# One attention and mixture-of-experts kernel: its order planner gets measured transfer lengths with a margin, its zero products another rule, and its order a new search

## The chip, the core and the metric

The program runs on one core of a Trainium2 chip. The core has five engines that work side by side and each take their instructions in program order: PE (matrix products), DVE (vector), ACT (scalar functions), POOL (general), and SP, which here only issues DMA transfers. The metric is the device time of one execution in microseconds (us). The kernel before was timed three times: 987.84, 989.49 and 993.25 us, median 989.49.

## The reference: what is computed

Attention over 8 batches, 12 heads, 448 positions and head width 64, with q and k normalised; its output, taken as 3584 tokens of 768 values, goes into a mixture of 8 experts, where each token uses the one expert of the greatest logit.

```python
q_n, k_n = (rmsnorm(q, g_q), rmsnorm(k, g_k))
scores = scale * np.matmul(q_n, k_n.transpose(0, 1, 3, 2))
scores = scores - np.max(scores, axis=-1, keepdims=True)
attn = np.exp(scores)
attn = attn / (np.sum(attn, axis=-1, keepdims=True) + 1e-09)
attn_out = np.matmul(attn, v)
...
x = np.ascontiguousarray(attn_out.transpose(0, 2, 1, 3)).reshape(B * S, H * D)
logits = x @ w_gate
e_idx = np.argmax(logits, axis=1)
...
for e in range(E):
    mask = e_idx == e
    h = np.maximum(x[mask] @ w1[e], 0.0)
    out[mask] = gate_w[mask, None] * eom[mask, e, None] * (h @ w2[e])
```

## The kernel before, in words

**Pairs of heads.** Attention is done in 48 pairs of heads, six to a batch. `pair_ops(i)` (before.py from line 509) writes down the steps of pair i, each with a name, an engine, a duration in ns that the planner counts with, the steps it needs, and the buffers it takes. The names are used below: `Lt` loads q and k (tile qkt); `sq`, `mh`, `ms` square and sum them; four small steps per group of pairs make the factor y; `n` and `qg` scale qkt; `hi` and `lo` split it into two halves of 16 bits (tile X); `Th` and `Tl` are the DMA transposes of the two halves into tile ss; `M0` to `M3` are products for the row maxima (psM), which DVE reduces in `x0` to `x3` (tile Z); `NT` and `nt` turn the maxima round; `S0` to `S3` are the scores (pss), six big and eight small products each; `e`, `f` on ACT take their exponentials and `p` forms the low half pl; `Lv`, `vh`, `vl` load and split v (tile vf). `A0` to `A6` multiply the exponentials with v into the one bank bank_a; the division of a pair is `av1`, `av2`, `av` on DVE (tiles rc and xr). bank_a is held from A0 of a pair until its `av`, so A0 of the next pair waits for that division. `tr`, `th`, `lg`, `la` make the router's logits, and `r<b>` finds the slots of batch b's tokens.

**The planner.** `Order.run` plays all these steps through, engine by engine, with the durations written down. Whenever an engine is free it takes, of the steps whose needs, buffers and transfers are due, the one with the smallest key. Keys come from the pair's number plus the numbers of the tables ORDER and SHIFT; SECOND says, pair by pair, on which of two engines a step runs. The program is then written out in the order in which the planner took the steps. No time of the planner is measured; it only settles what stands before what. A transfer is counted as a latency (`lat`) and a length on one common queue (`xfer`).

**Zero products.** Where the planner finds PE without work for longer than 400 ns between two steps, `run` puts n = (wait - 400) / 30 small products of a zero tile (nil, 56 columns, line 1456) behind the earlier step; they write columns 456 to 511 of bank_a, which the pairs' products don't use. 80 larger products of zeros (`w`, line 444) may run at the start wherever nothing else is due.

**After attention.** The first expert's products (g1e, line 1251) are part of the same plan. They need the tokens of that expert: route of batch 6 (r6), four scatters into a table (tab), a load from it (tie), three gathers (xge), a split (x16e) and three transposes (xTe). From there on a fixed order handles the other experts.

## Time and profile before

| | |
|---|---|
| median of three timed executions | 989.49 us |
| the profiled execution, device time | 990.61 us |
| its span in the trace | 988.6 us |
| outside the span | 2.0 us |
| PE busy | 934.8 us (95%) |
| DVE busy | 631.9 us (64%) |
| ACT, POOL busy | 549.7, 418.2 us (56%, 42%) |
| granted PE clock, mean over the span | 0.985 of full |

The table is read as averages over unlike stages: the first expert's products begin at 524.67 us, and up to there PE shares its time with three nearly full engines; behind it PE works with almost no pause. The busy time of PE holds the zero products too.

### The profile page before, as it was taken

The numbers are of one execution on the slowest core, as the hardware profiler recorded it, in microseconds if no ns is written. First come the engines' busy times: TensorE is split into PE (matmuls) and PEld (weight loads), VectorE is DVE, ScalarE is ACT, GpSimd is POOL, SyncE is SP. The second block draws the span as 40 slices with busy tenths as digits, with TensorE's granted clock in tenths as the row PEclk, the third lists the DMA queues.
The fourth block names the chain that finished last, engine by engine and source line by source line (L and its number), as shares of the span: only waits on it lengthen the run. The fifth ranks groups of instructions, "written<-read, shape, count | busy, mean of one in ns | idle before, by whom it ended". The sixth has DMA issues, their size and how long they took to land. (4 is left out here: it accounts for less than half of the span.)

```text
span 988.6 us, 29294 instructions
## 1 busy us (share of the span) xinstructions
PE 934.8 (95%) x12747; PEld 671.4 (68%) x12747; DVE 631.9 (64%) x1064; ACT 549.7 (56%) x809; POOL 418.2 (42%) x314
## 2 busy tenths in 40 slices
PE   5998999998899999999899999999999999999997
PEld 2576777776677777777676686686776767666664
DVE  6889899888787889896575456428336263536210
ACT  5876979878768677674582445324234252535110
POOL 3656768884766958644641313112121111101101
PEclk7999999999889999998999999999999999999999
DMA  6776969868659576564866599949738486667201
GB/s 169 137 195 135 209 141 165 199 115 174 110 114 218 107 170 123 128 93 75 171 194 206 144 268 265 203 108 237 192 105 238 117 232 187 180 211 218 69 1 47
DMA packets 182544, 157.44 MB, mean 159 GB/s; under 512 B 152448, under 2 KB 160262, under 8 KB 176268
## 3 DMA queue, kind: packets, MB, share of 16 engines
q1 hardware_dynamic: 176652, 133.28, 57.8%
q0 software_dynamic: 5760, 22.25, 7.1%
q8 instruction: 102, 1.67, 0.7%
q14 instruction: 30, 0.25, 0.1%
HBM read 96.73 MB, written 22.59 MB: 121 GB/s over the span
## 5 line engine op out<-in xcount | busy, mean ns | idle before, releaser
L667 POOL TENSOR_TENSOR pl<-p,ph 128x896 f16<-128x896 f32 x79 | 149.8, 1903 | 112.5 <-ACT ph L662 45.1
L613 DVE TENSOR_REDUCE Z<-psM 128x2 f16<-128x896 f32 x168 | 178.3, 1086 | 21.1 <-PE psM L598 16.2
L699 PE MATMUL bank_a<-vf,pf 128*128 128x65 f32 (+1 forms) x896 | 149.5, 280 | 8.1 <-DVE xr L717 8.1
L1266 POOL DMA_INDIRECT out<-oe,tie x24 | 27.7, 1155 | 254.4 <-DVE oe L1288 232.9
L640 PE MATMUL pss<-ss 64*128 64x448 f16 (+1 forms) x1152 | 127.0, 358 | 7.8 <-DVE pl L667 3.1
L699 PEld LDWEIGHTS bank_a<-vf,pf 128*128 128x128 f32 (+1 forms) x896 | 110.1, 180 | 26.5 <-issue 11.3
L1251 PE MATMUL g1e<-xTe,w0he 128*128 128x384 f16 x384 | 125.2, 326 | 0.0
L1253 PE MATMUL g1e<-xTe,w0le 128*128 128x384 f16 x384 | 125.2, 326 | 0.0
L1252 PE MATMUL g1e<-xTe,w0he 128*128 128x384 f16 x384 | 125.2, 326 | 0.0
L703 PE MATMUL bank_a<-vh,pl 128*128 128x65 f16 (+1 forms) x1088 | 123.0, 195 | 1.7 <-issue 1.7
L703 PE MATMUL bank_a<-vh,ph 128*128 128x65 f16 (+1 forms) x1088 | 122.6, 196 | 0.0
L701 PE MATMUL bank_a<-vl,ph 128*128 128x64 f16 (+1 forms) x1088 | 122.4, 193 | 0.0
L662 ACT ACTIVATE ph<-pss 128x896 f16<-128x896 f32 x112 | 101.8, 922 | 17.2 <-PE pss L646 17.2
L703 PEld LDWEIGHTS <-ph 128*128 128x128 f16 (+1 forms) x1088 | 110.2, 117 | 0.0
L703 PEld LDWEIGHTS <-pl 128*128 128x128 f16 (+1 forms) x1088 | 90.7, 101 | 1.8 <-issue 1.8
L701 PEld LDWEIGHTS <-ph 128*128 128x128 f16 (+1 forms) x1088 | 90.7, 103 | 0.0
L652 ACT ACTIVATE pf<-pss,lnv 128x896 f32<-128x896 f32 x56 | 56.6, 1010 | 50.2 <-PE pss L646 47.0
L658 ACT ACTIVATE p<-pss 128x896 f32<-128x896 f32 x79 | 72.2, 920 | 15.1 <-PE pss L646 12.0
L1253 PEld LDWEIGHTS <-w0le 128*128 128x128 f16 x624 | 60.7, 98 | 24.8
L1251 PEld LDWEIGHTS <-w0he 128*128 128x128 f16 x624 | 60.7, 98 | 23.7
L1252 PEld LDWEIGHTS <-w0he 128*128 128x128 f16 x624 | 60.7, 98 | 23.6
L646 PEld LDWEIGHTS <-sel 64*128 64x128 f16 (+1 forms) x1536 | 53.2, 99 | 31.3 <-issue 3.3
(328 smaller groups left out, 2300.8 us busy)
## 6 DMA issues: line engine op xcount, KB each, us to landing
wste<-w SPq DMA_DIRECT2D x48, 1024.0 KB, 5.8
qkt<-qkt SPq DMA_DIRECT2D x48, 448.0 KB, 4.4
vf<-v SPq DMA_DIRECT2D x48, 260.0 KB, 3.4
xs<-xr SPq DMA_DIRECT2D x16, 576.0 KB, 3.5
ss<-X SPq DMA_TRANSPOSE x96, 4.3
xs<-xr SPq DMA_DIRECT2D x16, 96.0 KB, 4.3
tab<-val,slot POOLq DMA_INDIRECT x32, 4.9
xge<-xs,tie POOLq DMA_INDIRECT x24, 4.9
```

Source lines behind the costliest of these rows:

```text
L613: V.tensor_reduce(out=o, in_=m, op=ALU.max, axis=AX.X, negate=True)
L640: T.matmul(out, lhsT=side(wk, 1, h, 128 * u, n, x), rhs=side(wq, 0, h, 0, S, x), start=k == 0, stop=False)
L652: A.activation(out=t, in_=st[f"S{u}"], func=AF.Exp, bias=self.lnv)
L658: A.activation(out=t, in_=st[f"S{u}"], func=AF.Exp)
L662: A.activation(out=t, in_=st[f"S{u}"], func=AF.Exp)
L667: return (V if eng == DVE else Pl).tensor_tensor(out=t, in0=st[f"e{u}"], in1=at[f"ph{u}"], op=ALU.subtract)
L699: T.matmul(out, lhsT=st[f"pf{u}"][:, k, q], rhs=vf[:, jv, :], **go)
L701: T.matmul(out[:, 0:D], lhsT=at[f"ph{u}"][:, k, q], rhs=vl[:, jv, :], start=False, stop=False)
L703: T.matmul(out, lhsT=at[f"p{'hl'[w // 2]}{u}"][:, k, q], rhs=vh[:, jv, :], **go)
L1251: nc.tensor.matmul(o, lhsT=wh[:, sl], rhs=xT[:, 0, k, 0:n], start=k == 0, stop=False)
L1252: nc.tensor.matmul(o, lhsT=wh[:, sl], rhs=xT[:, 1, k, 0:n], start=False, stop=False)
L1253: q["mm"] = nc.tensor.matmul(o, lhsT=wl[:, sl], rhs=xT[:, 0, k, 0:n], start=False, stop=k == KD - 1)
```

## The change

The planner's rules and numbers change, and with them the order of nearly all steps before 524.67 us; the work of each step does not. Part by part:

- Transfers are counted longer in `lat` (`Lt`, `Th` 1400 ns more, `Lv`, `Tl` 1050 ns more, by the new table LATE) and with other lengths (`Lt` 1900 to 2450 and 1900 to 1700, `Th`, `Tl` 1700 to 2020 and 1250 to 1180, `Lv` 1200 to 765, `k.cst` 546 to 1600, the loads of weights `ld` 2000 to 2500 or 5000, the store `st`). Two durations change as well: `S3` 960 to 700, `lg` 380 to 460.
- Zero products are now put in only for waits of more than 800 ns, and never between a pair's last product A and its division: there they go behind the division (`pad`, in front of the next step).
- `k.zero`, which makes the zero tiles, waits for `ms.0`.
- ORDER, STICK, SECOND and SHIFT hold new numbers. SECOND moves steps between engines: by count, 14 half-tiles of `lo` and 7 `qg` go from DVE to POOL, 15 `th`, 8 `vh`, 2 `nt` from ACT to DVE, 3 `p` from POOL to DVE, 2 `sq` from ACT to POOL, and 2 `mh` more are made on POOL, each of which halves an `ms` on DVE.

```diff
-REST, BEAT = 400, 30
+REST, BEAT, GAP = 400, 30, 800
+LATE = dict(Lt=1400, Lv=1050, Th=1400, Tl=1050)
...
-    ("S0", 0.028, 0.084, 2293.989, 0.255),
+    ("S0", 0.087, 0.406, 914.631, 0.073),
...
-    "lo": "100010 110001 110110",
+    "lo": "100100 110000 111000",
...
-    "th": "001000 000111 010100",
+    "th": "011111 011111 000001",
...
-        op = dict(name=name, eng=eng, ns=ns, after=after, key=key, fn=fn, bufs=bufs, lat=ns if lat is None else lat, xfer=xfer, port=port)
+        op = dict(name=name, eng=eng, ns=ns, after=after, key=key, fn=fn, bufs=bufs, lat=ns if lat is None else lat + LATE.get(name[:2], 0), xfer=xfer, port=port)
...
-        last = None
+        last, held = None, {}
         for o in out:
-            if o["eng"] == PE:
-                if last and last["until"] >= WARM:
-                    last["still"] = max(0, int((self.start[o["name"]] - last["until"] - REST) / BEAT))
-                last = o
+            if o["eng"] != PE:
+                continue
+            nm, r = o["name"].split(".")
+            if last and last["until"] >= WARM:
+                a, b = last["until"], self.start[o["name"]]
+                end = done.get(f"av.{held['i']}", 0) if held.get("n") == 7 else 0
+                side = "pad" if end > a else "still"
+                n = int((b - max(a, end) - REST) / BEAT)
+                if n > (GAP - REST) / BEAT:
+                    last[side] = n
+                    if side == "pad":
+                        o["pad"] = last.pop("pad")
+            if nm[0] == "A":
+                held = {"i": r, "n": held["n"] + 1 if held.get("i") == r else 1}
+            last = o
...
-        self.order.add("k.zero", DVE, 330, [], -20, lambda: [nc.vector.memset(x, 0.0) for x in (self.zero, self.nil)])
+        self.order.add("k.zero", DVE, 330, ["ms.0"], -20, lambda: [nc.vector.memset(x, 0.0) for x in (self.zero, self.nil)])
...
-        do("Th", SP, 1235, "hi", lambda: flip(0), f"ss:S0,S1,S2,M0,M1,M2", 1700, 1250, more=["k.edges"])
+        do("Th", SP, 1235, "hi", lambda: flip(0), f"ss:S0,S1,S2,M0,M1,M2", 2020, 1180, more=["k.edges"])
...
-            do(f"S{u}", PE, 768 if u < 3 else 960, "Tl", lambda u=u: Sc(u), f"s:{'p' if near else 'e'}{u}" + ("" if u in whole or near else f",f{u}"), more=more)
+            do(f"S{u}", PE, 768 if u < 3 else 700, "Tl", lambda u=u: Sc(u), f"s:{'p' if near else 'e'}{u}" + ("" if u in whole or near else f",f{u}"), more=more)
...
-        do("Lv", SP, 475, "", lambda: self.loadv(i), f"vf:{As}", 2100, 1200, more=[f"Th.{i}"] * (i < 4) + [f"Lv.{i - 1}"] * (i > 0))
+        do("Lv", SP, 475, "", lambda: self.loadv(i), f"vf:{As}", 2100, 765, more=[f"Th.{i}"] * (i < 4) + [f"Lv.{i - 1}"] * (i > 0))
...
+        def still(n):
+            for _ in range(n):
+                nc.tensor.matmul(self.bank_a[:, 456:512], lhsT=self.nil, rhs=self.nil[:, 0:56], start=True, stop=True)
+
         for o in self.order.run():
+            still(o.get("pad", 0))
             o["ins"] = o["fn"]()
-            if o.get("still"):
-                for _ in range(o["still"]):
-                    nc.tensor.matmul(self.bank_a[:, 456:512], lhsT=self.nil, rhs=self.nil[:, 0:56], start=True, stop=True)
+            still(o.get("still", 0))
```

The tables' numbers tell a reader nothing; what they make of the order is seen at three places. In the program before stand 849 zero products at 41 places, 21 of them with more than 13 each, which is what the new limit of 800 ns asks for; in the changed program stand 382 at 8 places.

The first place is PE where the products of pair 0 end (vh_114, pl_3 are its operands; psM_4 are the maxima of pair 4). Before:

```order
L703 LDWEIGHTS pl_3_592
L703 MATMUL bank_a<-vh_114,pl_3_592 128x65
L1456 LDWEIGHTS nil
L1456 MATMUL bank_a<-nil 128x56
...
L598 LDWEIGHTS ss_111
L598 MATMUL psM_4_888<-ss_111 128x448
```

The zero products there are 52. After (psM_5 are the maxima of pair 5, pss_2 the scores S2 of pair 3):

```order
L715 LDWEIGHTS pl_3_899
L715 MATMUL bank_a<-vh_114,pl_3_899 128x65
L610 LDWEIGHTS ss_107
L610 MATMUL psM_5_1088<-ss_107 128x448
...
L652 LDWEIGHTS ss_110
L652 MATMUL pss_2_1092<-ss_110 128x448
```

The zero products are gone from between the last product and the division, and real products of later pairs stand in their place.

The second place is DVE at the start, from the maxima of pair 0 (psM0_0) to those of pair 1 (psM2_1 and so on). Before:

```order
L613 TENSOR_REDUCE Z0_112<-psM0_0_252 128x2
L495 SCALAR_TENSOR_TENSOR y02_262<-psy02_263,y02_262 128x28
L558 TENSOR_REDUCE ms03_294<-sq4_278 128x14
L613 TENSOR_REDUCE Z0_112<-psM3_1_303 128x2
L613 TENSOR_REDUCE Z0_112<-psM2_1_308 128x2
L613 TENSOR_REDUCE Z0_112<-psM1_1_330 128x2
```

After:

```order
L625 TENSOR_REDUCE Z0_112<-psM1_0_256 128x2
L570 TENSOR_REDUCE ms02_286<-sq2_222 128x14
L570 TENSOR_REDUCE ms02_286<-sq3_278 128x14
L512 SCALAR_TENSOR_TENSOR psy02_305<-psy02_305,mm02_302 128x28
L686 TENSOR_SCALAR vh0_114<-vf0_245 128x6x64
L507 SCALAR_TENSOR_TENSOR y02_304<-psy02_305,y02_304 128x28
L690 SCALAR_TENSOR_TENSOR vl0_318<-vf0_245,vh0_114 128x384
L574 TENSOR_TENSOR qkt3_224<-qkt3_224,y02_304 128x896
L574 TENSOR_TENSOR qkt2_188<-qkt2_188,y02_304 128x896
L625 TENSOR_REDUCE Z0_112<-psM2_1_334 128x2
L625 TENSOR_REDUCE Z0_112<-psM3_1_339 128x2
```

Two sums ms, the scalings n of pairs 2 and 3 and the split of v of pair 0 now stand ahead of pair 1's maxima, which NT of pair 0 needs.

The third place is SP where attention passes into the experts (vf46, vf47 are loads of v, wste0_0 to wste0_3 of the first expert's weights, tie0 the load of its token list). Before:

```order
L1122 DMA wste0_0_10612<-w 128x2048
L468 DMA vf46_10719<-v 128x520
L1122 ISA
L1122 DMA wste0_1_10836<-w 128x2048
L1187 ISA
L1187 DMA tie0_10858<-tab_87 128x6
L468 DMA vf47_10881<-v 128x520
```

After:

```order
L480 DMA vf46_10243<-v 128x520
L1121 TENSOR_LOAD est0_126
L1121 ISA x2
L1134 ISA
L1134 DMA wste0_0_10284<-w 128x2048
L480 DMA vf47_10480<-v 128x520
L1199 ISA
L1199 DMA tie0_10500<-tab_87 128x6
L1134 ISA
L1134 DMA wste0_1_10505<-w 128x2048
```

The last load of v now stands ahead of the token list, and the second weight load behind it.

## Rows read from the trace of the kernel before

**Rows 1.** The page's head and part 1, and the PE clock of its part 2.

```profile
span 988.6 us, 29294 instructions
...
PE 934.8 (95%) x12747; PEld 671.4 (68%) x12747; DVE 631.9 (64%) x1064; ACT 549.7 (56%) x809; POOL 418.2 (42%) x314
...
PEclk7999999999889999998999999999999999999999
```

**Rows 2.** Windows by stage: stretch, length, busy of each engine (instructions), clock, DMA.

```profile
core 0: us, PE busy (x) PEld busy (x) DVE busy (x) ACT busy (x) POOL busy (x), PEclk, DMA share, GB/s
...
18.14:50.27 32.13, 30.60 (x398) 16.80 (x399) 25.79 (x34) 24.64 (x42) 21.39 (x15) 0.96 0.78 169
50.27:132.50 82.23, 75.48 (x1515) 59.36 (x1512) 72.64 (x115) 64.72 (x102) 55.57 (x39) 1.00 0.74 169
132.50:476.80 344.30, 322.42 (x6071) 249.85 (x6067) 288.50 (x547) 253.34 (x389) 237.58 (x162) 0.98 0.68 141
476.80:524.67 47.87, 42.31 (x856) 35.40 (x857) 30.55 (x70) 31.12 (x42) 22.53 (x15) 1.00 0.67 161
524.67:988.60 463.93, 456.70 (x3894) 306.72 (x3889) 203.06 (x277) 165.06 (x218) 76.13 (x65) 1.00 0.62 171
```

**Rows 3.** The same windows for the zero products of line 1456 alone (PE first).

```profile
50.27:132.50 82.23, 10.05 (x318) 9.06 (x318) 1.00 0.74 169
132.50:476.80 344.30, 14.80 (x404) 12.67 (x404) 0.98 0.68 141
476.80:524.67 47.87, 1.29 (x31) 1.15 (x31) 1.00 0.67 161
```

**Rows 4.** Timelines of PE and DVE where pair 0's products end.

```profile
50.27 1.51 PE L1456 MATMUL bank_a<-nil 128*128 128x56 f16 x52
...
53.03 0.74 PE L640 MATMUL pss<-ss 64*128 64x448 f16 x6 [0.19 <-DVE pl L667]
...
51.82 0.17 DVE L708 TENSOR_SCALAR rc<-bank_a 128x7 f32<-128x7 f32 x1 [2.00 <-PE bank_a L1456]
51.90 1.08 DVE L667 TENSOR_TENSOR pl<-pss,ph 128x896 f16<-128x896 f32 x1
```

**Rows 5.** Waits: who waited for whom, us in total, times, longest us.

```profile
DVE rc L708 <- PE bank_a L1456: 15.8, 12, 2.3
...
PE bank_a L699 <- DVE xr L717: 8.1, 10, 1.4
```

**Rows 6.** Windows around one fall of the clock.

```profile
448.00:451.00 3.00, 1.48 (x28) 1.16 (x27) 1.39 (x3) 1.33 (x2) 2.68 (x3) 1.00 0.70 133
451.00:458.00 7.00, 7.00 (x74) 4.75 (x70) 4.09 (x7) 1.01 (x1) 3.37 (x3) 0.51 0.15 40
```

**Rows 7.** Timelines of the start: ACT, SP and PE.

```profile
5.94 3.59 ACT L418 ACTIVATE sel<-cst 64x896 f16<-64x896 f32 x4 [3.89 <-DMA cst<-cst]
...
14.91 1.34 SPq L583 DMA_TRANSPOSE ss<-X  x1
...
18.14 1.30 PE L598 MATMUL psM<-ss 64*128 64x448 f16 x6 [9.64 <-DMA ss<-X]
...
28.36 0.74 PE L640 MATMUL pss<-ss 64*128 64x448 f16 x6
```

**Rows 8.** Timelines of the passage to the experts: SP and POOL.

```profile
496.09 0.34 SPq L1187 DMA_DIRECT2D tie<-tab  x1
...
510.56 10.21 SPq L1229 DMA_TRANSPOSE xTe<-x16e  x3
...
485.63 0.94 POOL L907 DMA_INDIRECT tab<-val,slot  x1 [0.30 <-issue]
...
501.94 1.05 POOL L1167 DMA_INDIRECT xge<-xs,tie  x1
```

**Rows 9.** Groups by line: busy us, mean ns, idle before.

```profile
L562 DVE TENSOR_TENSOR qkt<-qkt,y 128x896 f32<-128x896 f32 x13 | 14.1, 1084 | 0.2
...
L579 POOL TENSOR_TENSOR X<-qkt,X 128x512 f16<-128x512 f32 x48 | 54.9, 1168 | 23.7 <-ACT X L575 16.4 <-DVE qkt L567 4.4 <-DVE X L579 2.9
```

**Rows 10.** Timeline of POOL and DVE at 4 us.

```profile
4.27 1.68 POOL L548 TENSOR_TENSOR sq<-qkt 128x896 f32<-128x896 f32 x1 [1.12 <-DMA qkt<-qkt]
4.35 1.69 DVE L387 SCALAR_TENSOR_TENSOR g<-g 128x64 f32<-128x64 f32 x1 [3.11 <-DMA g<-g]
```

More of the change, by code (lines that the diff above doesn't have):

```diff
@@ L96 @@
[L96 to L104 removed]
+    ("Lt", -143.566, -2.599, -5.432, -540.431),
+    ("sq", 21.478, 260.723, -2.442, -4.286),
@@ new lines @@
+    ("S1", -0.753, -2.653, 1.814, 0.507),
+    ("e1", -5.012, -9.133, -78.580, -1.555),
+    ("f1", 45.591, 80.499, 2.750, 282.554),
+    ("p1", -10.779, -479.574, -0.837, -5.998),
+    ("S2", 0.361, -268.125, 761.608, -0.146),
+    ("e2", 0.590, 0.217, -0.295, -77.854),
+    ("f2", 492.464, -6.874, -2.358, 8.845),
+    ("p2", -0.157, -4.862, 6.450, -334.562),
+    ("S3", -0.404, -3.721, -88.741, -11.806),
+    ("e3", 2.875, -295.217, 0.259, -95.968),
+    ("f3", 1.227, -5.176, 0.517, -59.448),
@@ L114 @@
 NEAR = 600
-STICK = 13.704
+STICK = 17.407
 ENGINES = {
@@ L152 @@
 SHIFT = {
[L153 to L205 removed]
+    "k.cst": 1.890,
+    "k.gd": -7.174,
+    "k.wg": 1834.163,
+    "k.blank": 8.509,
+    "k.xs": -0.643,
+    "k.tab": 253.430,
+    "k.g": 6.916,
+    "k.ltri": -135.711,
+    "k.flat": 1834.299,
+    "k.edges": -3.322,
+    "s0": -217.527,
+    "r": 3.147,
+    "st": -51.735,
+    "s": 5.395,
+    "r-2": -389.627,
+    "r-1": 1.828,
+    "open1": -143.709,
+    "open2": -0.351,
+    "ld0": 186.479,
+    "wh0": -27.917,
+    "wl0": 7.119,
+    "ld1": -3.648,
+    "wh1": 521.013,
+    "wl1": 1834.536,
+    "ld2": -0.410,
+    "ti0": -28.414,
+    "xg0": 722.092,
+    "xh0": -168.958,
+    "xl0": 0.636,
+    "xt0": -0.927,
+    "ti1": -40.812,
+    "xg1": 2.384,
+    "xh1": 276.109,
+    "xl1": -40.787,
+    "xt1": -1.880,
+    "ti2": -44.374,
+    "xg2": -154.895,
+    "xh2": -218.624,
+    "xl2": 3.935,
+    "xt2": -1702.015,
+    "units": 379.907,
+    "g1": 738.894,
+    "hh": 276.860,
+    "hl": -40.053,
+    "g2": -41.049,
+    "o0": 2.855,
+    "o1": 519.464,
+    "sc": -183.618,
+    "k.id": 847.914,
+    "k.sel0": 0.035,
+    "k.sel1": -302.842,
+    "k.zero": 6.453,
+    "w": 253.289,
 }
@@ L400, in flat @@
             V.memset(self.lnv, math.log(SV))
-        add("k.cst", SP, 475, [], -14.5, load(st, io["cst"]), (), 2000, 546)
+        add("k.cst", SP, 475, [], -14.5, load(st, io["cst"]), (), 2000, 1600)
         add("k.gd", SP, 475, [], -10.5, load(self.g, io["g"]), (), 2000, 60)
@@ L411, in consts @@
         add("k.tab", SP, 475, ["k.blank", "av.0"], 2, table, (), 2000, 742)
-        add("k.g", DVE, 129, ["k.gd"], -10, scale)
+        add("k.g", DVE, 129, ["k.gd"], -10, scale, port=True)
         def sel(h):
@@ L423, in consts @@
         add("k.ltri", DVE, 135, ["k.cst"], -4, copy(self.ltri, st[:, 128:256]))
-        add("k.flat", DVE, 330, ["k.cst"], -4, flat)
+        add("k.flat", DVE, 330, ["k.cst"], -4, flat, port=True)
     def attn_alloc(self):
@@ L446, in attn_alloc @@
         for k in range(IDLE):
-            after = [f"w.{k - 1}"] if k else ["k.zero", "ms.0"]
+            after = [f"w.{k - 1}"] if k else ["k.zero"]
             self.order.add(f"w.{k}", PE, 213, after, 1000, lambda k=k: idle(k), [] if k else [("a", [f"w.{IDLE - 1}"])])
@@ L842, in pair_ops @@
         if i == last:
-            do("lg", PE, 190 * LGN, "", lg, "m:la", more=["k.wg"] + [f"th.{i - k}" for k in range(LGN)])
+            do("lg", PE, 230 * LGN, "", lg, "m:la", more=["k.wg"] + [f"th.{i - k}" for k in range(LGN)])
             do("la", DVE, 180, "lg", la)
@@ L1044, in attention @@
             pairs = range(NP * b, NP * b + NP)
-            self.order.add(f"st.{b}", SP, 1950, [f"av.{i}" for i in pairs], NP * b + NP + 2, lambda b=b: self.store(b), (), 2000, 4400)
+            self.order.add(f"st.{b}", SP, 3400, [f"av.{i}" for i in pairs], NP * b + NP + 2, lambda b=b: self.store(b), (), 1670, 5500)
     def plan(self):
@@ L1394, in moe @@
                 rel = [f"wl{m}.{2 * j + k}" for k in range(2) if 12 * m + 2 * j + k < 12 + EARLY] if m < 2 else []
-                add(f"ld{m}.{j}", SP, 475, after, n + 0.2 * j + 3 * m - 1 + 2000 * ((m, j) == (1, 2)), lambda m=m, j=j: load(m, j), [("wst", rel)], 2000, 3475)
+                add(f"ld{m}.{j}", SP, 475, after, n + 0.2 * j + 3 * m - 1 + 2000 * ((m, j) == (1, 2)), lambda m=m, j=j: load(m, j), [("wst", rel)], 5000 if (m, j) == (0, 0) else 2500, 3475)
             for x in range((12, EARLY, 0)[m]):
```

168 lines of the change are left out of this document (51 added, 117 removed).

## The prediction

> **What bounds the kernel now.** I read the page's head first, then windows by stage, then the zero products in the same windows, the waits, and timelines at a few places. PE is busy for 934.8 us of 988.6, DVE for 631.9 [rows 1], so PE looks like the bound; the reader should not stop there, because that busy time holds products of zeros. The windows [rows 2] split the span by places in the program: pair 0's last product (50.27), the first route (132.50), the seventh (476.80), the first expert's first product (524.67). In the last stage PE works 456.70 of 463.93 us and nothing of the change touches its order but a few loads, so I leave it as it is. The question is what lies between 18.14 us, the first real product [rows 7], and 524.67.
>
> In each of these stages I take the length less PE's busy time as idle and add the time of zero products [rows 3], since both are time in which PE has nothing real to do:
> - 50.27 to 132.50: 82.23 - 75.48 + 10.05 = 16.8 us
> - 132.50 to 476.80: 344.30 - 322.42 + 14.80 = 36.7 us
> - 476.80 to 524.67: 47.87 - 42.31 + 1.29 = 6.9 us
>
> Together 60 us of 474. DVE is the second in line: 72.64 of 82.23 us (88%) in the first of these stages, 288.50 of 344.30 (84%) in the second [rows 2]. So no order can shorten the first by more than 82.23 - 72.64 = 9.6 us as long as DVE's work is the same.
>
> What the zero products do there is shown by one place [rows 4]. Behind pair 0's last product 52 of them run for 1.51 us; rc, the division's first step, reads bank_a, comes behind them, and DVE stands idle for 2.00 us before it; the pl that is queued behind rc on DVE comes late in turn, and PE's next scores wait 0.19 us for it. In sum DVE waited 15.8 us in 12 such cases, and PE 8.1 us in 10 cases for the xr that ends a division [rows 5].
>
> **The change part by part.** I make the sum against the profiled execution, 990.6 us; the median of the three timed runs, 989.5, is 1.1 below it.
>
> *Work of the engines.* By the counts in the section on the change, 14 half-tiles of lo go to POOL at 1.168 us each [rows 9], 16.4 us, and with the other moves POOL gets some 24 us more, ACT some 15 less, DVE about 1 more. POOL's busy time is 42% of the span and ACT's 56% [rows 1], and in the two long stages POOL has 69% at most and ACT 79% [rows 2], so neither becomes the bound: cost nothing, hidden by PE. If that cover went, POOL's 24 us would be the price. PE's real products are the same in kind and number.
>
> *Start.* Two things pull apart. The four sel on ACT, 3.59 us from 5.94, stood ahead of everything that pair 0 needs of ACT [rows 7]; in the changed order its square, now on ACT, comes first and half of the sel later, so its first transpose can go out before 14.91. Against that, DVE now makes two n of 1.084 us [rows 9] and some smaller steps ahead of pair 1's maxima, which the first scores (28.36 before [rows 7]) need. And 291 of the 382 zero products that are left stand ahead of pair 0's first product with v, where 40 stood before. At 10.05 / 318 = 0.032 us each [rows 3] 291 are 9.2 us of PE, against 1.3: at worst the start gets 8 us longer. At best nothing: the steps that DVE takes earlier are missing later. I take the middle, +4 us.
>
> *Waits in the long stages.* Compared like with like, places of more than 13 zero products, the stage to 132.50 held 301 products at such places and has none after; the stage to 476.80 held 296 and has 35. At the prices of [rows 3] (0.032, and 14.80 / 404 = 0.037 us) that is 9.5 us of PE, and 10.8 less 1.3, again 9.5. These are places where PE had nothing due and where the new order puts other pairs' products. I count -7 us in the first stage, where DVE's 9.6 us are the limit. In the second -9.5, and -2.5 for divisions that come sooner, part of the 8.1 us of [rows 5]: -12 us. Bounds: 0, if other waits take their place, and -9.6 and -36.7, if PE never waits. I stay near the rows' 9.5, since the 21.9 us of plain idle time in the second stage stand where no zero products were, so that the planner did not see these waits before and may not now. The longer transfer lengths work on these: a load or transpose that is asked for earlier is seldom late; I give that no extra us.
>
> *Zero products taken away, and the clock.* From 451 to 458 us the granted clock was 0.51, behind a stretch of 3 us in which PE was busy 1.48 us [rows 6]; 6.8 us at half rate cost 3.4 us. There were three such falls, and the mean of 0.98 over 344.30 us [rows 2] puts them at some 7 us. With fewer long waits I expect one fall less, rounded down: -2 us; bounds -7 and +7 (two more falls).
> [...]
>
> *Passage to the experts.* The first expert cannot begin before a chain: last scatter 485.63, list load issued 496.09, first gather 501.94, transposes from 510.56 for 10.21 us [rows 8], first product 524.67. That is 39 us, most of it transfers that the change does not touch. PE loses 6.9 us in this stage, but if it comes sooner it meets that chain. -2 us; bounds -6.9, and +3 if PE waits there for what it now does before. The later second weight load and the earlier load of v in SP's queue lie inside this chain's waits.
>
> *k.zero, wst and k.cst numbers:* they only move steps of the first 20 us or DMA issues with slack; nothing.
>
> Sum: +4 - 7 - 12 - 2 - 2 = -19 us; 990.6 - 19 = 971.6, on the median's scale 971 us.
>
> **The rivals.**
> *DVE takes over (time 983).* It is at 84 to 88% where PE is to be packed tighter, and instructions of POOL can hold it: at 4.35 us a DVE instruction on 64 columns took 1.69 us beside a 1.68 us one of POOL [rows 10]. The change adds 22 POOL instructions net; if half of them each hold a DVE instruction for 1.168 us [rows 9], that is 13 us, of which I count 12 on the path since DVE has little room: 971 + 12 = 983. For it: the shares. Against it: the n on DVE averages 1.084 us over 13 [rows 9], so such blocking is rare so far.
> [...]
> *No change (991).* The zero products only marked waits whose cause stays: waits move, none goes; the start's +4 and half the clock's gain stay. 990.6 + 4 - 2 less 1.1 is 991. For it: 21.9 us of idle time had no zero products. Against it: the places fell from 18 to 2 in the long stages.
> *Slower, by the clock (1005).* Fillers are gone at 33 places while unplanned waits stay, and the clock falls after each cluster of them. Price 3.4 us a fall. From 971 it takes seven falls more than the three of now to pass 995; ten more give 1005. For it: each fall so far stood behind waits without fillers. Against: in the stage to 132.50, with its 6.8 us of idle time, the clock stayed at 1.00 [rows 2].
>
> **How the numbers follow.** I give the forecast 0.60 (956 to 984 by itself), DVE 0.15, no change 0.12, the clock 0.13. A measurement of this kernel tells about 0.5%, 5 us, from no change: faster means under 984.5, slower over 994.4. All of the first and two thirds of DVE's are faster, 0.70; the rest of DVE's and no change are the same, 0.17; the clock slower, 0.13. The range leaves out the clock's 0.13, some of no change and some of sums with most terms at their best: 953 to 991.
>
> **What would show it.** Right: idle time plus zero products between pair 0's last product and the first expert near 40 us instead of 60; rc waiting for zero products hardly ever; pair 0's last product some 4 us after 50.27; the last stage near 464. Wrong: the first real wait of PE for xr or pl grows past 8 us (DVE), half-clock stretches by the dozen (clock), or a stall of over 3 us right before the first expert (chain). If the sum fails it is most likely in the start, whose term is the least bound, or in the second stage.

## The result and the profile after

The changed kernel takes 995.39 us in the median of 20 executions (986.81 to 1001.62), the kernel before 988.66 (985.46 to 993.25) beside it: 1.0055 of before, 95% interval 1.0034 to 1.0077. It is slower by half a per cent; forecast were 971 us and a range that ends at 991. The ratios here and below are estimated from the executions of both kernels without the few slow ones, and so are not the quotients of the medians beside them (here 1.0068). Its profiled execution has this head:

```profile
span 994.7 us, 28334 instructions
...
PE 936.7 (94%) x12280; PEld 669.1 (67%) x12280; DVE 633.9 (64%) x1071; ACT 537.2 (54%) x782; POOL 439.5 (44%) x336
...
PEclk9997997999999989999999999999999999999999
```

Behind its first slice the line of the granted clock has three dips, as in [rows 1], but they stand earlier and two of them are deeper (7 for 8). The windows by stage, cut at the same places of the program as [rows 2] (pair 0's last product, first route, seventh route, first expert), and below them the zero products of line 1467 in the three middle ones, which answer to [rows 3]:

```profile
17.80:57.44 39.64, 34.39 (x612) 23.18 (x611) 33.40 (x47) 25.01 (x43) 27.16 (x21) 0.96 0.76 154
57.44:130.80 73.36, 65.01 (x1072) 49.47 (x1069) 63.75 (x101) 52.99 (x79) 49.51 (x34) 0.88 0.69 160
130.80:484.00 353.20, 327.73 (x5882) 249.43 (x5880) 294.48 (x562) 256.84 (x388) 260.95 (x181) 0.96 0.71 141
484.00:530.96 46.96, 41.94 (x793) 35.45 (x790) 30.45 (x66) 29.10 (x40) 20.90 (x14) 0.96 0.72 165
530.96:994.70 463.74, 456.52 (x3895) 306.71 (x3891) 203.89 (x279) 163.89 (x217) 74.76 (x65) 1.00 0.60 171
...
57.44:130.80 73.36, 0.00 (x0) 0.00 (x0) 0.88 0.69 160
130.80:484.00 353.20, 1.24 (x35) 1.10 (x35) 0.96 0.71 141
484.00:530.96 46.96, 0.00 (x0) 0.00 (x0) 0.96 0.72 165
```

Three things are to be seen. The last stage is as long as before, so all of the loss lies ahead of 530.96. Pair 0 ends 7.2 us later. And from there to the first expert the idle time and the zero products together are 38.84 + 1.24 = 40 us, where they were 60, yet that stretch is only 0.9 us shorter (473.52 for 474.40): PE's real products take longer there, and the clock column says why, 0.88 and 0.96 for 1.00 and 0.98. The first fall of the clock behind pair 0, by windows, and another one further on:

```profile
57.00:70.00 13.00, 9.42 (x179) 7.00 (x178) 11.56 (x21) 9.69 (x13) 7.44 (x5) 1.00 0.66 198
70.00:84.00 14.00, 13.03 (x122) 9.69 (x124) 10.65 (x19) 6.47 (x13) 5.88 (x5) 0.51 0.69 151
...
152.00:166.00 14.00, 12.67 (x106) 8.57 (x108) 8.28 (x11) 4.45 (x8) 12.79 (x11) 0.51 0.86 153
166.00:170.00 4.00, 4.00 (x68) 3.44 (x64) 3.59 (x5) 3.96 (x5) 0.97 (x1) 1.00 0.73 138
```

PE is busy for 9.42 of the 13 us ahead of the fall, with no zero product in them; then half rate for 14 us. Behind pair 0 there are seven such stretches up to the first expert, 47.8 us in all; before had three, 17.1 us. The waits ahead of the first, in PE's timeline:

```profile
57.44 0.36 PE L610 MATMUL psM<-ss 64*128 64x448 f16 x2
58.91 0.74 PE L652 MATMUL pss<-ss 64*128 64x448 f16 x6 [1.10 <-ACT pf L664]
59.48 0.38 PE L658 MATMUL pss<-nt,sel 64*128 64x128 f16 x8
60.77 0.33 PE L711 MATMUL bank_a<-vf,pf 128*128 128x65 f32 x1 [0.92 <-DVE xr L729]
```

**One sum for every trace.** Pair 0's end is a poor mark, since the new order puts products of pairs 2 to 5 ahead of it. So below each trace is taken from its first real product (M) to the first expert's first product, cut at 60 us, and split from the records of the single products into *waits* (no real product in flight: idle or zeros), *half-rate loss* (half of the time that real products take while the clock is at half), and the rest, the real products' length at the full clock. In the changed kernel's trace the 16-bit products into bank_a start 0.056 us apart from 71.86 to 72.31 us, at half clock, and 0.030 us apart from 85.70 to 85.85 us, at the full one.

| us | whole | waits to 60 | waits behind | half-rate loss to 60 | behind | products at full clock |
|---|---|---|---|---|---|---|
| before | 506.5 | 15.2 | 52.2 | 0.7 | 8.3 | 430.2 |
| changed | 513.9 | 22.0 | 38.6 | 1.4 | 22.9 | 429.0 |

The products at the full clock are the same. Waits: 6.8 more in the start, 13.6 fewer behind. Half-rate loss: 15.4 more. In sum 7.4 more, less 1.1 because the first product comes earlier (17.01 for 18.14): the 6.3 us by which 530.96 is later than 524.67.

The 20 executions of the changed kernel say the same without a trace: the fastest has a mean granted clock of 0.983 and takes 986.81 us, one of 0.969 takes 999.46; a line through all of them falls 8 us per 0.01 of clock.

### The profile page after: what moved, and what is told of

Same layout as the page of the kernel before. It is cut to its first block, busy times and chain, and to the rows that moved or that the text cites. A ratio compares the mean times of both kernels' runs of the same rounds, so it can differ in the third digit from the quotient of the medians.

```text
span 994.7 us, 28334 instructions
## 1 busy us (share of the span) xinstructions
PE 936.7 (94%) x12280; PEld 669.1 (67%) x12280; DVE 633.9 (64%) x1071; ACT 537.2 (54%) x782; POOL 439.5 (44%) x336
## 5 line engine op out<-in xcount | busy, mean ns | idle before, releaser
L679 POOL TENSOR_TENSOR pl<-p,ph 128x896 f16<-128x896 f32 x76 | 142.9, 1889 | 99.6 <-ACT ph L674 25.0
L711 PE MATMUL bank_a<-vf,pf 128*128 128x65 f32 (+1 forms) x896 | 154.2, 287 | 5.3 <-DVE xr L729 5.3
L652 PE MATMUL pss<-ss 64*128 64x448 f16 (+1 forms) x1152 | 129.8, 365 | 8.6 <-DVE Z L625 3.5
L711 PEld LDWEIGHTS bank_a<-vf,pf 128*128 128x128 f32 (+1 forms) x896 | 113.7, 186 | 24.2 <-issue 11.5
L715 PE MATMUL bank_a<-vh,pl 128*128 128x65 f16 (+1 forms) x1088 | 126.7, 198 | 1.8 <-POOL pl L679 1.8
L715 PE MATMUL bank_a<-vh,ph 128*128 128x65 f16 (+1 forms) x1088 | 126.9, 199 | 0.0
L713 PE MATMUL bank_a<-vl,ph 128*128 128x64 f16 (+1 forms) x1088 | 126.2, 196 | 0.0
L674 ACT ACTIVATE ph<-pss 128x896 f16<-128x896 f32 x112 | 102.0, 918 | 21.6 <-PE pss L658 21.6
L715 PEld LDWEIGHTS <-ph 128*128 128x128 f16 (+1 forms) x1088 | 113.3, 120 | 0.0
L713 PEld LDWEIGHTS <-ph 128*128 128x128 f16 (+1 forms) x1088 | 93.1, 105 | 0.0
L670 ACT ACTIVATE p<-pss 128x896 f32<-128x896 f32 x76 | 69.5, 916 | 41.6 <-PE pss L658 41.5
L591 POOL TENSOR_TENSOR X<-qkt,X 128x512 f16<-128x512 f32 x62 | 70.3, 1156 | 27.7 <-issue 13.8
L658 PEld LDWEIGHTS <-sel 64*128 64x128 f16 (+1 forms) x1536 | 54.1, 100 | 30.7 <-issue 3.5
```

The lines of the kernel that those rows point to most:

```text
L591: return [E.tensor_tensor(out=X[:, 1, :, :, d], in0=x, in1=X[:, 0, :, :, d], op=ALU.subtract) for x, d in sides(self.qkt.pop(i))]
L652: T.matmul(out, lhsT=side(wk, 1, h, 128 * u, n, x), rhs=side(wq, 0, h, 0, S, x), start=k == 0, stop=False)
L670: A.activation(out=t, in_=st[f"S{u}"], func=AF.Exp)
L674: A.activation(out=t, in_=st[f"S{u}"], func=AF.Exp)
L679: return (V if eng == DVE else Pl).tensor_tensor(out=t, in0=st[f"e{u}"], in1=at[f"ph{u}"], op=ALU.subtract)
L711: T.matmul(out, lhsT=st[f"pf{u}"][:, k, q], rhs=vf[:, jv, :], **go)
```

## The experiments

My theory was: the waits went as forecast, but those that are left have no products in them, so the clock falls behind them. The rivals: the new order itself stretches the products (contention, transfers), or zeros cost what they save. The executions fell on five more chips; before was timed on each beside them and took 986 us on one of them and 996 to 999 on the others, so every ratio is to before on the same chip. "Clock" is the median over a kernel's executions; in brackets stands that of the one execution that was traced, from which the last two columns come. Where the two differ, the columns don't stand for the median: e4 is the worst case.

| kernel | before there (its clock) | time | ratio (95%) | clock (traced) | waits to 60 / behind | half-rate loss to 60 / behind |
|---|---|---|---|---|---|---|
| e1_zeros_as_before | 996.4 (0.987) | 997.7 | 1.0018 (0.9992 to 1.0043) | 0.991 (0.994) | 24.3 / 51.6 | 1.6 / 2.6 |
| e2_zeros_before_division | 996.4 (0.987) | 1001.5 | 1.0063 (1.0040 to 1.0087) | 0.986 (0.988) | 22.5 / 53.0 | 1.4 / 8.3 |
| e4_zeros_at_measured_waits | 996.4 (0.987) | 1011.3 | 1.0163 (1.0123 to 1.0204) | 0.977 (0.985) | 24.2 / 53.9 | 1.6 / 7.2 |
| e5_order_before_new_zeros | 996.4 (0.987) | 993.5 | 0.9964 (0.9936 to 0.9991) | 0.978 (0.982) | 16.8 / 46.1 | 0.7 / 11.8 |
| e6_before_free_banks | 999.2 (0.985) | 1003.4 | 1.0038 (1.0008 to 1.0069) | 0.973 (0.970) | 16.0 / 50.7 | 0.7 / 22.9 |
| e7_measured_waits_free_banks | 999.2 (0.985) | 1011.0 | 1.0114 (1.0064 to 1.0163) | 0.978 (0.974) | 23.3 / 55.4 | 2.1 / 17.9 |
| e8_old_rule_free_banks | 999.2 (0.985) | 1010.8 | 1.0105 (1.0065 to 1.0145) | 0.974 (0.973) | 24.0 / 52.0 | 1.6 / 22.5 |
| after_again | 986.4 (0.988) | 997.0 | 1.0097 (1.0066 to 1.0127) | 0.973 (0.977) | 23.8 / 37.0 | 1.5 / 20.1 |
| e9_measured_waits_newton_in_psum | 986.4 (0.988) | 984.2 | 0.9977 (0.9957 to 0.9998) | 0.987 (0.990) | 22.0 / 40.0 | 2.6 / 5.0 |
| e10_old_rule_newton_in_psum | 986.4 (0.988) | 986.6 | 1.0003 (0.9976 to 1.0030) | 0.984 (0.980) | 23.2 / 34.7 | 1.7 / 15.2 |
| e12_no_zeros | 986.4 (0.988) | 985.4 | 0.9990 (0.9964 to 1.0016) | 0.975 (0.973) | 18.2 / 35.0 | 7.9 / 13.4 |
| e13_order_before_measured_waits | 996.2 (0.986) | 995.1 | 1.0005 (0.9980 to 1.0030) | 0.979 (0.978) | 15.4 / 48.8 | 0.7 / 15.2 |
| e15_order_before_no_zeros | 996.2 (0.986) | 993.5 | 0.9982 (0.9955 to 1.0009) | 0.975 (0.973) | 15.2 / 45.7 | 0.6 / 20.2 |
| e16_no_zeros_in_the_start | 996.2 (0.986) | 999.9 | 1.0037 (1.0002 to 1.0071) | 0.973 (0.978) | 19.4 / 44.9 | 5.2 / 13.1 |
| e9_again | 996.2 (0.986) | 995.1 | 1.0005 (0.9978 to 1.0032) | 0.986 (0.986) | 23.1 / 44.8 | 1.7 / 9.9 |
| after_third | 998.4 (0.985) | 995.7 | 0.9965 (0.9937 to 0.9993) | 0.980 (0.977) | 23.1 / 41.8 | 1.7 / 18.1 |
| e12_again | 998.4 (0.985) | 991.0 | 0.9926 (0.9893 to 0.9959) | 0.978 (0.963) | - | - |
| e17_measured_waits_none_in_the_start | 998.4 (0.985) | 996.6 | 0.9998 (0.9975 to 1.0021) | 0.981 (0.984) | 19.6 / 46.4 | 5.1 / 6.5 |

The products at the full clock are 428.7 to 434.2 us in all of these traces; of e12_again, whose traced execution was the slowest of its nine (1003.1 us), no trace is used.

**e1 and e2: the zero rule undone, whole and in part.**

```diff
-REST, BEAT, GAP = 400, 30, 800
+REST, BEAT, GAP = 400, 30, 400        # e1 only
-                end = done.get(f"av.{held['i']}", 0) if held.get("n") == 7 else 0
+                end = 0                # e1 and e2
```

> The changed kernel's order with the zero rule of before: every planned wait of TensorE over 400 ns is filled behind the earlier step, also between a pair's last product and its division (1186 zero products in 48 groups, where the changed kernel has 382 in 8). Theory (the clock): the changed kernel lost its gain because waits without zeros let the clock fall; here the half-clock time between pair 0's last product and the first expert goes from 47.8 us to under 25, the real products there from 433.4 us to 414 to 422, but idle time and zeros come back to about 55, so the whole is 985 to 1000. Rival (the order): the new order's own waits on transfers and on DVE stretch that stage whatever stands in them; the half-clock time stays near 48 us and the whole goes to 1000 to 1015, since the division waits again.

> The changed kernel with one part of its zero rule undone: zeros may stand between a pair's last product and its division again, only waits over 800 ns are filled (1022 zeros in 26 groups). Theory (the clock): the long fall at 70 us, which stands behind the planned waits of 2.5, 2.0 and 1.6 us behind pairs 0 and 1 that this part left empty, is gone, and the one at 97 us too; half-clock time 25 to 35 us, real products 418 to 427 us; the division's wait for zeros costs some of it; whole 983 to 998. Rival (the order): falls stay at these places, whole 996 to 1010.

In e1 the clock came back as the theory says, to 0.991 beside before's 0.987, in e2 to 0.986: 2.6 and 8.3 us of loss behind 60 us for 22.9, and the fall at 70 us is gone in both. But the waits behind rose to 51.6 and 53.0 us, against 38.6 in the changed kernel and 41.8 in after_third, whose chip is like theirs; so the whole was not better. The old rule is no cure: it buys the clock at its price in waits.

**e4: zeros at 18 waits of the changed kernel's own trace**, 10 to 88 of them at each.

```diff
+FILL = {"M0.5": 25, "S2.3": 18, "M1.5": 22, "M1.4": 12, "M2.8": 45, "A2.9": 80, ...}
-            still(o.get("still", 0))
+            still(max(o.get("still", 0), FILL.get(o["name"], 0)))
```

> The changed kernel with zeros added at 18 places where its own trace has TensorE waiting over 0.6 us with none (539 zeros more, each group about 0.3 us shorter than the measured wait). Theory (the clock): nearly all falls behind pair 0 go, half-clock time under 15 us, real products 414 to 420 us, idle time and zeros near 42, so the whole is 978 to 987, below before. Rival (contention): the real products are longer because the other engines and the transfers are in their way, not by the clock's falls; the granted clock rises but the products stay above 428 us and the whole at 992 to 998.

The traced execution lost 7.2 us, as expected, but it had a clock of 0.985; the median of the six is 0.977, no higher than the changed kernel's on other chips, so here zeros did not hold the clock. And the waits did not stay at 42: 53.9 (41.8 in after_third). The timeline of DVE and PE at the first place, where the changed kernel waited 1.10 us, shows why:

```profile
60.06 0.15 DVE L721 TENSOR_SCALAR rc<-bank_a 128x7 f32<-128x7 f32 x1
...
60.27 1.09 PE L1468 MATMUL bank_a<-nil 128*128 128x56 f16 x25 [2.07 <-DVE rc L721]
61.30 1.30 PE L653 MATMUL pss<-ss 64*128 64x448 f16 x6
```

The zeros write bank_a, whose pair waits for its division; they stand 2.07 us for DVE to read it, and the scores queued behind them on PE stand too: 3.10 us of wait instead of 1.11. The wait grew likewise at 68.3 (3.23 for 1.05), 94.1 (4.66 for 1.88) and 181.6 (2.87 for 1.28), while 88 zeros at 363, where no division was pending, waited for nobody. But there the wait became their own length: 2.31 us, where the three traces of the changed kernel, whose product waits for a transfer, have 3.29, 2.73 and 0.91.
That the zeros write columns 456 to 511, where nothing of the pair stands, did not spare them this wait of 2.07 us.

**e5: the order of before with the changed kernel's zero rule** (the end of `run` and `still` as in the change, tables and costs of before).

> The kernel before, its order untouched, with the changed kernel's zero rule (177 zeros in 7 groups where before has 849 in 41). Theory (the clock): idle time and zeros between pair 0's last product and the first expert go from 60.35 us to 38 to 48, half-clock time there from 17 us to 35 or more, real products from 414 us to 425 or more; the gain and the loss about cancel: 984 to 998. Rival (the order is what lets the clock fall): the old order keeps its clock, half-clock time stays under 25 us, and the whole goes to 968 to 978.

As the theory had it: waits behind 60 us fell by 6.1, the loss rose by 3.5 (against before's trace, which is from another chip); it is slightly faster than before. The clock fell from before's 0.987 to 0.978 on one chip, with the order untouched.

**e6, e7, e8: zeros only in a bank without a pending reader**, for the order of before, for e4 and for e1.

```diff
+            k = "m" if hold["a"] and late["m"] <= t else "a"
+            if late[k] > t:
+                return
+            z = self.bank_a[:, 456:512] if k == "a" else self.ps_m.tile([128, 512], F32, tag="m", ...)[:, 0:56]
...
-            t["t"] = self.ps_m.tile([128, 512], F32, tag="m", name=f"psy{b}{c}")[:, 0:n]
+            t["t"] = self.f2.tile([128, n], F32, tag="psy", bufs=BUFS["y"], name=f"psy{b}{c}")
```

> The kernel before, its order and its planned waits untouched; zero products are written into bank_a only while no division of it is pending, else into the bank of NT, tr and lg when that is free, else left out (482 zeros in 20 groups, before has 849 in 41); the Newton step's tile moves from that bank to SBUF. Theory (zeros beside a pending division make waits, and those elsewhere keep the clock for nothing): idle time and zeros behind 60 us fall from 52 us to 42 to 46, half-rate loss stays at 8 to 12 us, whole 5 to 9 us below before. Rival (zeros cost nothing, the waits come from the order): no change within 3 us.

> As the kernel with zeros at the measured waits, but each group goes where no division is pending (bank_a, or the bank of NT, tr and lg), and is left out where neither is free (856 zeros in 22 groups); the Newton step's tile is in SBUF. Theory (the clock falls for want of products, and zeros cost time only where they stand in bank_a beside a pending division): idle time and zeros behind 60 us go from 53.9 us back to 38 to 43, the real products' loss to half rate stays under 10 us, whole 12 us or more below the changed kernel, 978 to 988 beside a kernel before at 989. Rival (zeros cost what they take wherever they stand): idle time and zeros stay at 50 to 55, the whole stays above before by 1% or more.

> The changed kernel's order with the zero rule of before, each group in a bank without a pending division or left out (873 zeros in 35 groups; the same rule in bank_a alone had 1186 in 48). Theory: loss to half rate behind 60 us 3 to 10 us as under that rule, idle time and zeros there 40 to 45 us instead of 51.6, whole 6 to 12 us below that kernel and as much below the changed one. Rival (zeros cost what they take wherever they stand): the same time as under the old rule in bank_a, 0.2% above before.

All three were slower than before, against my expectation. For e7 and e8 the cause is the second edit, which I had taken for free and which moves the tile psy of the factor y from PSUM to SBUF: e9 and e10 below, without it, have ratios 1.0 to 1.4% lower, on another chip. In e6 DVE's steps on psy took 7 us more in all than in before, but its clock was lower too, and no run tells the two apart. e7's timeline of DVE and POOL, and DVE's group of that line in e7:

```profile
279.08 4.63 DVE L513 SCALAR_TENSOR_TENSOR psy<-psy,mm 128x42 f32<-128x42 f32 x1 [1.60 <-ACT psy L505]
279.55 1.88 POOL L680 TENSOR_TENSOR pl<-p,ph 128x896 f16<-128x896 f32 x1
281.40 2.25 POOL L592 TENSOR_TENSOR X<-qkt,X 128x512 f16<-128x512 f32 x2
...
L513 DVE SCALAR_TENSOR_TENSOR psy<-psy,mm 128x42 f32<-128x42 f32 (+2 forms) x18 | 10.8, 601 | 6.4 <-ACT psy L505 6.4
```

With its tile in SBUF a step on 42 columns takes 4.63 us and ends at 283.71, just behind three instructions of POOL that run beside it (the last ends at 283.65); in e7 the 18 steps of this line take 601 ns in the mean, with the tile in PSUM 198 ns, in the changed kernel as in e9. PE's NT waited 3.93 us for DVE there, and the clock fell again during that wait, at 283.4 us. Ahead of that place e7 was as the theory has it: the waits from 58 to 91 us had the lengths of the changed kernel's, and the half-rate stretches from 70 to 183 us were gone.
That POOL's instructions held the step is my reading of these times; why they would is not shown.

**e9, e10 and e12, with the changed kernel once more beside them.** e9 and e10 are e7 and e8 without that second edit, with 1 us of planned time between the last reader of that bank and zeros in it; e12 has none of the 382 zeros (the 80 `w` of the start stay).

```diff
+            k = "m" if hold["a"] and late["m"] <= t - 1000 else "a"      # e9, e10
...
-            still(o.get("pad", 0))       # e12: still(0), both calls
-            still(o.get("still", 0))
```

> The changed kernel once more, unchanged, on the same chip as the next three, so that their times can be set beside it. Both theories expect what it gave: 0.3 to 0.8% above before.

> The changed kernel with zeros at 14 of the 18 measured waits, each group in bank_a or in the bank of NT, tr and lg, whichever has no reader pending (796 zeros in 20 groups); the Newton step's tile stays in PSUM, since the run with it in SBUF showed a step of 0.2 us standing for 4.6 us beside GpSimd. Theory (falls for want of products; zeros cost time only beside a pending reader of their bank): idle time and zeros behind 60 us 38 to 45 us, the loss to half rate there under 12 us against 22.9, whole 0.8% or more below the changed kernel beside it. Rival (filling moves the waits elsewhere, the falls with them): idle and zeros over 48 or the loss still over 16 us, the whole within 0.4% of the changed kernel or above.

> The changed kernel's order with the zero rule of before, each group in a bank without a pending reader or left out (606 zeros in 25 groups), the Newton step's tile in PSUM. Theory: idle and zeros behind 60 us 38 to 46 us (51.6 under the old rule in bank_a alone), loss to half rate 8 to 16 us, whole 0.3 to 1.2% below the changed kernel. Rival (filling moves the waits elsewhere): the whole within 0.3% of the changed kernel or above.

> The changed kernel without any of its 382 zero products (291 of them stand before 50 us). Theory (zeros hold the clock, the start's waits come from the order): idle time and zeros before 60 us stay at 21 to 24 us, with the zeros turned into idle time; the clock falls in the start at two or three more places and the real products there grow by 2 to 6 us; whole 2 to 8 us above the changed kernel. Rival (the start's zeros themselves hold up the division and the first products): the wait before 60 us falls under 18 us and the whole is 3 us or more below the changed kernel.

On this chip e9 decides for the theory: 12.8 us below the changed kernel, at a clock of 0.987 for 0.973. Its trace against after_again's, first real product to first expert: 500.7 for 511.6 us, of which the half-rate loss is 14.0 less (7.6 for 21.6), the waits 1.3 and the products 1.9 more. Windows and PE's timeline of e9 at the first place:

```profile
57.00:70.00 13.00, 11.70 (x265) 9.51 (x260) 10.96 (x18) 8.51 (x14) 7.44 (x5) 1.00 0.84 190
70.00:84.00 14.00, 11.86 (x204) 9.29 (x199) 13.96 (x27) 10.64 (x19) 6.38 (x5) 1.00 0.83 181
...
59.57 0.82 PE L1479 MATMUL z<-nil 128*128 128x56 f16 x25
60.74 0.74 PE L653 MATMUL pss<-ss 64*128 64x448 f16 x6 [0.35 <-ACT pf L665]
```

The scores start 1.10 us behind the end of the M ahead (59.64), 1.11 in the changed kernel, and the 14 us behind 70 are at the full clock. e10 came 10.4 us below the changed kernel, as expected; in its trace the half-rate loss is 4.7 us less than in after_again's and the waits are 2.8 us less.

e12 is the miss: I expected it 2 to 8 us above the changed kernel, it is 11.6 below. Its half-rate loss is after_again's (21.3 for 21.6), only moved: the start's rose by 6.4 and the rest fell by 6.7. Its waits are shorter, by 5.6 before 60 us and 1.9 behind. So the rival held for the start: the 291 zeros there make waits themselves. Windows of e12:

```profile
38.30:55.30 17.00, 12.11 (x107) 6.12 (x105) 14.39 (x18) 12.86 (x19) 13.84 (x10) 0.60 0.67 154
55.30:70.00 14.70, 12.39 (x258) 10.13 (x260) 12.56 (x20) 9.88 (x16) 7.43 (x5) 1.00 0.60 155
70.00:84.00 14.00, 10.86 (x171) 8.10 (x167) 14.00 (x27) 10.71 (x19) 5.81 (x5) 1.00 0.79 186
```

Nearly the same four waits as in the changed kernel (1.10, 0.91, 1.00 and 0.70 us from 60 to 73 us; there 1.11, 0.92, 1.05 and 0.70), in both without zeros, and no fall behind them, where the changed kernel's clock falls at 70.2 us; here it had been at half in most of the 17 us ahead (0.60 in the mean).
The changed kernel's own traces differ in this too: around the same four waits its clock fell at 70.2 and at 70.8 us, for 13.7 us, in two of them, and at 60.8 and 74.4 us, for 6.8 and 3.4 us, in after_third.

**e13, e15, e16 and e9 again: order or zeros?** e13 is the order of before with zeros at 28 measured waits in free banks, e15 the order of before without zeros, e16 the changed kernel with `still(o.get("still", 0) * (o["until"] > 55000))`.

> The kernel before, its order untouched, with few zeros (the changed kernel's rule) and zeros added at 28 places where its own trace under that rule has TensorE waiting over 0.6 us, each group in a bank with no reader pending or left out (504 zeros in 22 groups). Theory (the falls come from waits without products, in either order alike): idle time and zeros behind 60 us stay at 44 to 48 us, the loss to half rate goes from 11.8 us to 4 to 8, whole 4 to 9 us below before. Rival (the new order is the better one once its clock is held): 0.2% or more above the changed order filled in the same way, that is, at before or above.

> The kernel before, its order untouched, without any zero products (before has 849). Theory (the new order is no shorter than the old; the falls cost it): real products lose 15 to 25 us to half rate in all, idle time 47 to 55 us, whole within 0.7% of before on either side, and within 0.5% of the changed order without zeros, which gave 0.999 of before. Rival (the new order is worth the 1% that its waits are shorter): 0.7% or more above the changed order without zeros, that is, 0.6% or more above before.

> The changed kernel without the 291 zero products that stand before 55 us; the 20, 15 and 56 behind them stay. If the 11 us of the kernel without any zeros came from the start (a clock that falls there once more does not fall at 70 us, or the division waits less), this kernel gives the same: 0.8 to 1.3% below the changed one, with the long half-rate stretch at 70 us gone. If it came from the 35 zeros behind, it stays within 0.4% of the changed kernel.

> The changed kernel with zeros at the measured waits in free banks once more, on the chip of these three. Theory: 0.1 to 0.5% below before again, with under 12 us lost to half rate. Rival (that the first run's falls were few by chance): at before or above.

Without zeros the old order is at 0.9982 of before, the new at 0.9990 on its chip: neither the order nor before's 849 zeros is worth what can be measured here. The clock, though, goes with before's zeros and not with the order: on one chip each, the old order has 0.986 with its 849 zeros and 0.975 with none, the new one 0.975 with none beside before's 0.988. The time stays the same, so before's zeros cost in waits about what they save at the clock. e16 lost the stretch at 70 us as expected, with some 4 us less wait in the start, but not the time that I expected: waits behind 60 us were 44.9. e9's half-rate loss stayed low (9.9) and its clock at 0.986, but its waits behind were 44.8 for 40.0 on the other chip, and it is no faster than before (0.1 to 0.5% were expected); the changed kernel was not timed on this chip. e13 missed its 4 to 9 us too: at 28 places it held the clock only in part (15.2). Its ratio is that of e9 beside it, 1.0005: filled by the same rule, the two orders are even.

**after_third, e12 again and e17** (e9 without the start's zeros).

> The changed kernel a third time, beside the next two on one chip, since before itself has taken 986 us on some chips and 996 on others. Expected 0.3 to 1.0% above before; wait before 60 us 22 to 24 us, loss to half rate 20 to 25 us.

> The changed kernel without any zeros again, beside the changed one. If the 1.1% that it gained over the changed kernel is the start's (waits before 60 us 18 us against 22 to 24, the fall at 70 us moved ahead to 48 us), it comes again: 0.5% or more below the changed kernel, waits before 60 us under 20 us, loss to half rate in all within 4 us of the changed kernel's. If it was chance, within 0.4% of the changed kernel.

> The changed kernel with both: no zeros before 55 us, and zeros in free banks at the measured waits behind (505 in 15 groups). If the two causes add, the waits before 60 us are 18 to 20 us and the loss to half rate behind 60 us is under 12 us: 0.2 to 0.6% below the kernel without zeros, 0.8 to 1.6% below the changed one. If the start's zeros are needed to hold the clock, the loss to half rate before 60 us takes back what the waits give, and it stays 0.2% or more above the run with the start's zeros kept (0.998 and 1.0005 of before).

On this chip the changed kernel is 0.35% faster than before, where I had expected 0.3 to 1.0% above it: not because it gained, its time is 995 to 997 on all three chips, but because before takes 998.4 here. e12 is below the changed kernel again, by 4.7 us in the medians and 0.4% in the ratios: less than the 0.5% that I had asked for and at the edge of what I had called chance. e17 is not: its trace has 8.2 us less half-rate loss than after_third's, but that is the fastest of its 12 executions, and in the median its clock is hardly higher (0.981 for 0.980). The two causes do not add up.

No kernel beats both beyond doubt. e9 does so on the chip where before takes 986 us, by 0.2%, and is even with before on another; e12 is below the changed kernel on both chips where they ran side by side.

## Why the prediction was wrong, by its own steps

**Waits: right by their own measure, a third too large as a gain.** -21 us of idle time and zeros were forecast behind pair 0 (the terms -7, -12 and -2); 60.3 went to 40.1, -20.3. But 6 us of before's 26 us of zeros lay under the end of the real product ahead of them and held nothing up: counted where no real product is in flight, as in the table, the waits behind pair 0 fell from 54.1 to 39.9. The signs that I had named for being right came out, these 40 us, rc and the last stage, and the time did not: none of them looks at the length of the real products. rc no longer waits for zeros (the line of rows 5 is gone; DVE now waits 13.5 us in 10 cases for the pairs' own products):

```profile
DVE rc L720 <- PE bank_a L715: 13.5, 10, 4.6
...
PE bank_a L711 <- DVE xr L729: 5.3, 7, 1.4
```

**Clock: the step that failed.** "With fewer long waits I expect one fall less", -2 us with bounds of -7 and +7; it was +15.4. The waits that the new order removed were those that the old one had filled with zeros: 25 of the 26 us of zeros went, while the idle time without any product grew from 34.2 to 38.8 us in the same stretch [rows 2, 3]. With that the falls came, as I had written in the rival ("each fall so far stood behind waits without fillers", that is, without zero products) and not carried into the sum. It was the rival of 0.13, right in kind and in price (half of a stretch's length): 47.8 for 17.1 us at half rate, 15.4 us of loss, is four and a half of its falls of 3.4 us where it counted ten, and that was enough because the other terms gave less. What spoke against it, the stage with 6.8 us of idle time at a clock of 1.00, was a stage whose zeros took 10.05 us [rows 2, 3]. That the clock is the loss is shown by the sum over the two traces and by the spread of the changed kernel's own executions; that zeros hold it, by the clocks of e1, e5 and e15 beside before's (0.991, 0.978 and 0.975 for 0.987, 0.987 and 0.986) and by e9 beside the changed kernel's (0.987 for 0.973), each on one chip. That filling the waits gains time is shown on e9's first chip alone.

**Start: right in kind, mis-sized.** +4 us was the term, pair 0's end came 7.2 later, inside the bounds of 0 to +8. The runs without zeros there (e12, e16, e17: waits of 18.2 to 19.6 us for 22.0 to 23.8) give the zeros some 4 us, which the forecast had at most at 9.2 - 1.3 = 7.9; they save as much at the clock (1.4 to 1.7 us of loss for 5.1 to 7.9). The rest is the order: the first transpose goes out 3 us earlier, as expected, but pair 1 is later. The changed kernel's ACT, SP and PE there:

```profile
10.67 1.15 ACT L587 ACTIVATE X<-qkt 128x512 f16<-128x512 f32 x2 [1.09 <-POOL qkt L579]
19.34 1.15 ACT L587 ACTIVATE X<-qkt 128x512 f16<-128x512 f32 x2 [2.85 <-POOL qkt L579]
...
11.85 1.34 SPq L595 DMA_TRANSPOSE ss<-X  x1
...
17.01 0.74 PE L610 MATMUL psM<-ss 64*128 64x448 f16 x6
...
30.16 1.30 PE L652 MATMUL pss<-ss 64*128 64x448 f16 x6
```

Pair 1's split (the second line) waits for POOL's scaling, and the first scores stand at 30.16 for 28.36 [rows 7].

**The rest.** DVE did not take over: PE's waits for xr fell from 8.1 to 5.3 us (the second line above; [rows 5]), and the products' length at the full clock is unchanged, 429.0 for 430.2. The passage gave 0.9 us for the 2 forecast (46.96 for 47.87), the last stage nothing, as forecast. One slip of the working: the rival of no change says that half the clock's gain stays but subtracts the whole 2 us; with half it comes to 992, above the top of the range.

**What stays open.** Why the clock falls behind some clusters of waits and not behind others, and why before, and not the changed kernel, is 10 us slower on some chips; before was not traced there. The changed kernel's waits are longer there too, but on after_third's chip its clock was higher, 0.980 in the median for 0.973 and 0.975; at 8 us per 0.01 that is worth 4 to 6 us, by my estimate, and about covers them.

## What to carry to other kernels

Where TensorE's granted clock falls as it does here, judge an order by the idle time in which no product runs, not by its waits in all: this order took 25 of 26 us of zeros out behind pair 0, let the idle time there grow from 34.2 to 38.8 us, and from the first real product to the first expert lost 15.4 us at the clock for 6.8 us less of waits. Put a filler where nothing else waits for its bank: in e4 the zeros in bank_a stood 2.07 us for DVE and passed the wait on to the scores queued behind them, 3.10 us for 1.11; and 88 zeros, sized by one trace's wait of 3.29 us, were a wait of 2.31 us in themselves, where another execution of the changed kernel has 0.91. And where a kernel's own executions spread by more than 1% with the granted clock, as the changed kernel's do (986.81 us at 0.983 to 1001.62 at 0.966), one trace of it is one draw: compare the clock of all executions, on one chip.

## What the runs showed that I had not expected

On every chip where before takes 996 us or more the traces hold waits that no instruction of the program ends ("remote"), and on the two others none. All ten traces of the new order on those chips have them between 394 and 413 us and again between 488 and 508 us, and near the second place the clock falls for 6.8 or 10.2 us; in e1 that is all of the half-rate time behind 60 us. In after_third two of DVE's waits come close together, the first put down to a product that had long ended, the second to none; ACT stands to about the same times (vh at 491.61, ph at 493.19):

```profile
491.61 0.17 DVE L720 TENSOR_SCALAR rc<-bank_a 128x7 f32<-128x7 f32 x1 [2.07 <-PE pss L658]
491.69 0.15 DVE L945 TENSOR_REDUCE second<-most 128x1 f32<-128x8 f32 x1
493.05 1.10 DVE L625 TENSOR_REDUCE Z<-psM 128x2 f16<-128x896 f32 x1 [1.20 <-remote]
```

PE's next product waited 4.80 us there for 1.36 in after_again, and the clock was at half from 494 us. What stops the engines is not shown by these traces. It is part of why waits behind 60 us are some 3 to 5 us longer on those chips in one and the same kernel (41.8 for 37.0 and 38.6; 44.8 for 40.0).

On after_third's chip the changed kernel is the faster one at the same granted clock: its execution at 0.983 takes 993.09 us, before's four at 0.983 take 998.09 to 1002.65. On the chip of after_again no execution of the two kernels has the same clock: 0.968 to 0.977 for the changed one, 0.984 to 0.993 for all but one of before's.
